# The six loads of batch 0's k move from SyncE's queue to ScalarE's

## The chip, the cores and the metric

The kernel runs on one core of a Trainium2 chip. The metric is the device time of one launch in microseconds, the median over runs. Six queues of work matter on the core: TensorE (PE, with its weight loads PEld), VectorE (DVE), ScalarE (ACT), GpSimd (POOL), SyncE (SP), which only issues DMAs, and the 16 DMA engines that all issued transfers share. ScalarE can issue DMAs too; an issue takes its place in ScalarE's own order of instructions.

## What is computed

Softcapped attention over 4 batches of 12 heads, 448 positions and 64 values per head, then a feed-forward block with a leaky activation on the 1792 tokens that come out:

```python
scores = scale * np.matmul(q, k.transpose(0, 1, 3, 2))
scores = cap * np.tanh(scores / cap)
scores = scores - np.max(scores, axis=-1, keepdims=True)
attn = np.exp(scores)
attn = attn / (np.sum(attn, axis=-1, keepdims=True) + 1e-09)
x = np.matmul(attn, v)            # heads side by side: 1792 x 768
h = x @ w_in                      # 768 x 2048
g = np.maximum(h, 0.0) + alpha * np.minimum(h, 0.0)
out = g @ w_out                   # 2048 x 768
```

q, k, v and cap are float32; w_in and w_out come in 8 bytes per value and are brought to float32 on the chip.

## The kernel before

Heads are worked on in pairs, six per batch. For batch 0 the q and k of each pair are loaded as 112 partitions of 2 x 256 values (`loads32`, line 467), 224 KB per load, into the tiles `wp4` to `wp7` (three pairs to a tile). TensorE turns them against the identity (line 543), ScalarE or VectorE copies the result out of PSUM (lines 425 and 427), and TensorE multiplies (scores, line 578). ScalarE then takes the tanh (line 615), VectorE the maximum of it (line 619), ScalarE the exponential (line 626), TensorE turns the result (line 730) and multiplies by v (line 793). Beside this, w_in comes in 16 chunks of 768 KB (issue at line 1048); VectorE brings each to float32 in three passes (lines 1060, 1064, 1070), it is scaled and split, and once all are there the first feed-forward product (line 959) can run, batch by batch, with the attention of the next batch between; the second product (line 1000) follows.

The order of all of this is made by a planner, `Plan`. Each step is handed to `op` with a priority, with its time on each engine that could do it, and with what it reads and writes. `order` (line 140) plays the program through with these times: each engine takes, of the steps that are ready, the one of lowest priority. Where TensorE has nothing ready it gets a small filler matmul on the identity (line 1235). `emit` (line 275) then calls the steps in this order, under a schedule in which every engine keeps the order it was given. So the order is fixed when the program is built, fillers included; at run time each instruction waits for what it needs.

A load is an `op` for SyncE alone, with an issue time, a delay and a transfer time of the planner's model (`load`, line 457). Its priority is a sum of a constant, of the pair, and of an entry of the list `OFF` (line 85) chosen by `plan.tag`: entries 155, 157, ... are those of k, and 156, 158, ... those of q, for pairs 0 to 5. This gives the order k of pair 1, k of pair 0, q of pairs 0, 1 and 3, then the first chunk of w_in, k of pairs 3 and 2, and then v, the rest of q and k, and further chunks of w_in mixed.

Before the planned part, ScalarE issues the load of `cap` into 128 partitions (line 1238, tile `small`), VectorE computes its reciprocal, and ScalarE loads two of the values into registers:

```python
nc.scalar.dma_start(out=capt, in_=cap.to_broadcast([P, 1]))
...
nc.scalar.load(capr, capt[:1].bitcast(I32))
nc.scalar.load(icapr, icap[:1].bitcast(I32))
all_ops()
with tc.manual_schedule():
    plan.emit()
```

Of the kernel before, what the change touches and what calls it, by code (L numbers as in the profile page):

```python
# [39 lines left out]
QK_P = -455.54  # L40
# [3 lines left out]
A_S = 17.19  # L44
# [43 lines left out]
class Handle:  # L88


    def __init__(self, kind):
        self.kind, self.ops, self.slot = kind, [], None


class Plan:
# [4 lines left out]

    def __init__(self):
        self.ops, self.acc, self.line = [], {}, []
        self.fill, self.fill_until = None, 0.0
        self.tag = -1

    def handle(self, kind):
# [5 lines left out]
    def op(self, prio, times, fn, r=(), w=(), rows=1.0, port=True, mode=0, first=0.0):  # L112
        o = lambda: None
        o.first = first
        o.prio, o.times, o.fn, o.rows, o.idx, o.port, o.mode = prio + OFF[self.tag], times, fn, rows, len(self.ops), port, mode
        o.handles, deps = [], set()
        for write, regions in ((False, r), (True, w)):
            for x in regions:
                if isinstance(x, Handle):
                    if x not in o.handles:  # L120
                        o.handles.append(x)
                        x.ops.append(o)
                    x = (x, 0, 1)
                space, lo, hi = x
                old = self.acc.setdefault(space, [])
                deps.update(e[2] for e in old if e[0] < hi and lo < e[1] and (write or e[3]))
                if write:
                    old[:] = [e for e in old if e[0] < lo or hi < e[1]]
        for write, regions in ((False, r), (True, w)):
            for x in regions:  # L130
                space, lo, hi = (x, 0, 1) if isinstance(x, Handle) else x
                self.acc[space].append((lo, hi, o.idx, write))
        o.deps = len(deps)
        o.next = []
        for d in deps:
            self.ops[d].next.append(o)
        self.ops.append(o)
        return o
# [134 lines left out]
        return started  # L273

    def emit(self):
        for _, fn, e in self.order():
            fn(e)

# [2 lines left out]
def kernel(  # L281
# [11 lines left out]
    nc = tc.nc  # L293
# [76 lines left out]
    plan = Plan()  # L370
    op = plan.op
# [82 lines left out]
    def heads(src, b, pair):  # L454
        return src[b, 2 * pair:2 * pair + 2].rearrange("h (p c) d -> p h (c d)", c=NCH)

    def load(prio, dst, src, b, pair, w):
        op(prio, {"sp": (600, 1400, 940)}, lambda e: nc.sync.dma_start(out=dst.rearrange("p (h c) -> p h c", h=2),
                                                          in_=heads(src, b, pair)), w=w)

    class Unit:
        pass
# [2 lines left out]
    raw32, qT, v0 = {}, {}, {}  # L465

    def loads32():
        for pair in range(NPAIR):
            n = 2 * NCH * D
            for i, src in ((4, k), (6, q)):  # L470
                o = pair % 3 * n
                t = wpair[i + pair // 3].rearrange("p a b -> p (a b)")[:CP, o:o + n]
                raw32[i, pair] = t, (("wp", i + pair // 3), o, o + n)
                qT[pair] = wpair[i + pair // 3].rearrange("p a b -> p (a b)")[:, o:o + S]
                plan.tag = 155 + 2 * pair + (i == 6)
                load(QK_P + A_S * pair, t, src, 0, pair, [raw32[i, pair][1]])
        vbatch(0)

    def vslot(b, pair):
# [24 lines left out]
    def vbatch(b):  # L504

        u = Unit()
        vb.append(u)
        t = vam[:, b % 2]
        u.vmx, u.inv, u.s = (t[:, NPAIR + i:NPAIR + i + 1] for i in range(3))
        u.osc, u.tok = small[:, 12 + b:13 + b], ("vam", b % 2)  # L510
        plan.tag = 142 + b
        prio = V_P if b == 0 else B1_P + (b - 1) * NPAIR * B_S - B_S
        op(prio, {"dve": 30}, lambda e: nc.vector.memset(t[:, :NPAIR], 0.0), w=[(u.tok, 0, 9)])
        tops = []
        for pair in range(NPAIR):
            rv, m = vslot(b, pair)
            v0[b, pair] = rv, m
            plan.tag = 167 + 6 * (b > 0) + pair if b < 2 else 142 + b
            load(prio + 0.4 * pair, rv, v, b, pair, [m])
            plan.tag = 142 + b  # L520
            if b < VM:
                tops.append((rv.bitcast(BF16).rearrange("p (c f t) -> p c f t", f=P, t=2), m))
                if len(tops) == (2 if b else NPAIR):
                    gram_v(prio + 0.4 * pair, t[:, pair:pair + 1], (u.tok, pair, pair + 1), tops)
                    tops = []
                continue
            op(prio + 0.4 * pair, {"dve": 680}, lambda e, pair=pair, rv=rv: absmax(t[:CP, pair:pair + 1], rv),
               r=[m], w=[(u.tok, pair, pair + 1)], port=False)
        prio += 3
        op(prio, {"dve": 80}, lambda e: nc.vector.tensor_reduce(out=u.vmx, in_=t[:, :NPAIR], axis=AX.X, op=ALU.max),  # L530
           r=[(u.tok, 0, 6)], w=[(u.tok, 6, 7)])
        first, *rest = pow2(u.inv, u.s, None)
        if b < VM:
            first, *rest = root(u.inv, lambda: nc.vector.reciprocal(out=u.s, in_=u.inv))
        allmax(prio, u.vmx, P, [(u.tok, 6, 7)], first, [(u.tok, 7, 9)])
        chain(prio, rest, w=[(u.tok, 7, 9)])
# [335 lines left out]
    def attention(b, pair, mate):  # L872
# [6 lines left out]
        for dst, src, w in ((rq, q, rqr), (rk, k, rkr)):  # L879
            if scores32:  # L880
                for h in range(2):
                    op(prio - 20, {"sp": LOAD_C}, lambda e, h=h, dst=dst, src=src: nc.sync.dma_start(
                        out=dst.rearrange("p (c h d) -> p h c d", h=2, d=D)[:, h],
                        in_=src[b, 2 * pair + h].rearrange("(p c) d -> p c d", c=NCH)), w=[(w[0], w[1] + h / 2, w[1] + (h + 1) / 2)])
            else:
                load(prio - 20, dst, src, b, pair, [w])
# [323 lines left out]
    def all_ops():  # L1210
        loads32()
        g_scales(2300)
        for part in range(2):
            attention_0(part)
        for j in range(0, NF, WG):
            w_in_chunks(j, WG)
        for part in range(2):
            mm1_batch(0, *PART[part], part)
        w_out_all()
        out_scale(0)  # L1220
        for b in range(1, B + 1):
            if b < B:
                vbatch(b)
                for pair in range(0, NPAIR, 2):
                    a = attention(b, pair, None)
                    units([a, attention(b, pair + 1, a)], S, ST1_P, finish)
                out_scale(b)
            mm2_batch(b - 1)
            if b < B:
                mm1_batch(b, 0, S, 0)  # L1230
# [52 lines left out]
```

## Time and profile before

| what | us |
|---|---|
| median of 3 runs | 666.45 (665.8 to 666.66) |
| the profiled execution's own time | 667.37 |
| its span, first to last instruction | 665.6 |

The profile is one execution recorded by the hardware profiler. A busy share of an engine is an average over the whole span, so the rows below are mostly of the first 60 us, where the loads in question are. A row of the timeline gives the start, the time taken (of the group, where like instructions were merged), and in brackets how long the engine was idle before it and what ended that. "SPq" and "ACTq" are issues of DMAs by those engines; the time of an issue is not the time of the transfer.

### The profile page before, as it was taken

Reading aid. Unit: us, or ns where it says so; the run is one execution under the profiler, and the core shown is the slowest. Engines: PE = TensorE matmul, PEld = TensorE weight load, DVE = VectorE, ACT = ScalarE, POOL = GpSimd, SP = SyncE. Lnnn points to the kernel's source line nnn. Section 1 sums busy time; section 2 is a strip of 40 time slices with the busy share of each in tenths; the row PEclk is TensorE's granted clock in tenths of the full one; section 3 lists DMA queues with packets and bytes.
Section 4 is the critical chain, followed back from the end, with each engine's and each line's share of the span. In section 5 each row is a group of like instructions: output and inputs, shape, how many; then the busy total and the mean of one; then the engine's idle time right before and its main releaser. Section 6 shows DMA issues by size and latency. Waiting matters only on the chain.

```text
span 665.6 us, 13056 instructions
## 1 busy us (share of the span) xinstructions
PE 642.9 (97%) x4934; PEld 406.2 (61%) x4934; DVE 469.8 (71%) x885; ACT 407.0 (61%) x839; POOL 245.8 (37%) x369
## 2 busy tenths in 40 slices
PE   9986999999999999999999999999999999999997
PEld 8864877888886655455455555544555555556664
DVE  3899999999999977989975877899994004440000
ACT  5876899988787877747853766778774113331000
POOL 1243457547764734635544321357451000000000
PEclk9997999999999999999999999999999999999999
DMA  9998863735753699948676899968667100000111
GB/s 221 286 274 231 258 188 103 225 107 151 148 89 63 156 164 197 169 99 157 116 156 155 162 175 178 185 120 165 113 116 131 33 19 24 1 1 1 37 35 25
DMA packets 190047, 87.05 MB, mean 131 GB/s; under 512 B 156256, under 2 KB 186272, under 8 KB 189984
## 3 DMA queue, kind: packets, MB, share of 16 engines
q1 hardware_dynamic: 189760, 86.12, 59.1%
q8 instruction: 39, 0.64, 0.4%
q14 instruction: 24, 0.20, 0.1%
q10 hardware_dynamic: 224, 0.10, 0.1%
HBM read 45.82 MB, written 5.51 MB: 77 GB/s over the span
## 4 chain that ended last, share of the span: by engine, by line
PE 55%; DMA 2%; DVE 2%; ACT 1%; issue 1%; SPq 0%; DVEq 0%; ACTq 0%
PE p L959 25%; PE p L1000 23%; PE p L776 4%; PE s L584 3%; DMA ptall<-pw 2%; DMA rqk<-in_k_dram 1%; DVE small L394 1%; DVE mxs L619 0%; DVE pw L441 0%; PE p L411 0%; ACT tall L626 0%; PE p L414 0%; DVE pw L435 0%; ACT tall L615 0%; DVE nat L438 0%
## 5 line engine op out<-in xcount | busy, mean ns | idle before, releaser
L959 PE MATMUL p<-xring,wi 128*128 128x448 f16 (+2 forms) x1440 | 224.3, 315 | 0.8 <-DVE iv_wi L388 0.8
L1000 PE MATMUL p<-wp,gall 128*128 128x384 f16 x1344 | 224.1, 326 | 0.1
L959 PEld LDWEIGHTS <-wi 128*128 128x128 f16 x1440 | 135.4, 98 | 83.7 <-issue 4.0
L1000 PEld LDWEIGHTS <-gall 128*128 128x128 f16 x1344 | 129.6, 98 | 89.9 <-issue 6.2
L626 ACT ACTIVATE tall<-tall,mxs 128x448 f32<-128x448 f32 x126 | 83.2, 666 | 18.9 <-POOL mxs L621 13.3
L969 DVE SCALAR_TENSOR_TENSOR gr<-p,ca_g,gr 128x448 f32<-128x448 f32 (+2 forms) x80 | 46.8, 585 | 52.5 <-ACT gr L431 51.7
L621 POOL TENSOR_SCALAR mxs<-mxs,small 128x2 f32<-128x2 f32 x70 | 43.6, 623 | 80.0 <-DVE mxs L619 66.8
L619 DVE TENSOR_REDUCE mxs<-tall 128x2 f32<-128x896 f32 x63 | 67.7, 1078 | 4.7 <-ACT tall L615 4.2
L441 DVE SCALAR_TENSOR_TENSOR pw<-tall,rr,pw 128x448 f16<-128x448 f32 x84 | 60.0, 725 | 8.6 <-ACT pw L431 7.9
L431 ACT ACTIVATE gr<-p,cs_g 128x448 f32<-128x448 f32 (+2 forms) x66 | 36.7, 557 | 37.1 <-PE p L959 36.0
L431 ACT ACTIVATE wp<-p,small 128x384 f32<-128x384 f32 x23 | 13.2, 576 | 62.2 <-PE p L1000 62.1
L615 ACT ACTIVATE tall<-s,ams 128x896 f32<-128x896 f32 x42 | 41.5, 999 | 12.3 <-PE s L584 5.7
L438 POOL TENSOR_TENSOR gall<-gr,gall 128x256 f16<-128x256 f32 (+4 forms) x50 | 37.2, 746 | 19.4 <-ACT gall L425 12.2
L645 POOL TENSOR_SCALAR rr<-sums 128x2 f32<-128x2 f32 (+2 forms) x70 | 23.1, 330 | 57.0 <-ACT tall L626 41.5
L425 ACT ACTIVATE gall<-gr 128x384 f16<-128x384 f32 (+4 forms) x58 | 26.6, 465 | 28.0 <-DVE gr L969 27.9
L435 DVE TENSOR_SCALAR wp<-p,joint 128x384 f32<-128x384 f32 (+1 forms) x2 | 1.0, 517 | 60.4 <-ACT wp L431 60.4
L431 ACT ACTIVATE pw<-tall,rr 128x448 f16<-128x448 f32 x46 | 30.3, 664 | 16.4 <-DMA ptall<-pw 9.9
L776 PE MATMUL p<-ptall,vs 112*64 112x448 f16 x384 | 39.4, 354 | 0.0
L438 DVE TENSOR_TENSOR gall<-gr,gall 128x384 f16<-128x384 f32 (+3 forms) x62 | 30.1, 486 | 4.7 <-ACT gall L425 1.8
L776 PEld LDWEIGHTS <-vs 112*64 112x64 f16 x384 | 21.2, 110 | 16.9 <-issue 5.1
L584 PE MATMUL s<-qkTs 64*128 64x448 f16 (+1 forms) x288 | 28.1, 352 | 0.6 <-ACT tall L615 0.6
L427 POOL CAST gall<-gr 128x192 f16<-128x192 f32 (+4 forms) x28 | 19.0, 681 | 24.4 <-DVE gr L969 22.5
(180 smaller groups left out, 943.3 us busy)
## 6 DMA issues: line engine op xcount, KB each, us to landing
wp<-in_moe_w_in_dram SPq DMA_DIRECT2D x16, 768.0 KB, 7.9
wp<-in_moe_w_out_dram SPq DMA_DIRECT2D x16, 768.0 KB, 4.9
rvs<-in_v_dram SPq DMA_DIRECT2D x38, 224.0 KB, 3.2
rqk<-in_k_dram SPq DMA_DIRECT2D x12, 224.0 KB, 3.2
rqk<-in_q_dram SPq DMA_DIRECT2D x12, 224.0 KB, 3.3
ptall<-pw SPq DMA_TRANSPOSE x128, 3.3
wp<-in_k_dram SPq DMA_DIRECT2D x6, 224.0 KB, 8.6
wp<-in_q_dram SPq DMA_DIRECT2D x6, 224.0 KB, 7.6
```

What stands on the lines that cost most here:

```text
L431: nc.scalar.activation(out=o, in_=i, func=AF.Copy, scale=s)
L438: (nc.gpsimd if e == "pool" else nc.vector).tensor_tensor(out=o, in0=a, in1=b, op=ALU.subtract)
L441: nc.vector.scalar_tensor_tensor(out=o, in0=i, scalar=s, in1=hi, op0=ALU.mult, op1=ALU.subtract)
L584: yield lambda z=z, w=w: nc.tensor.matmul(s[rows, x, :S], q[a, z * S + cols.start:z * S + cols.stop], q[a, w * S:(w + 1) * S], start=(z == ...
L615: op(pr, {"act": (152 if reg else 245) + 377 * 2}, lambda e: nc.scalar.activation(out=t, in_=s[:, :, :S].rearrange("p c (j k) -> p c j k", ...
L619: op(pr, {"dve": 136 + 469 * 2}, lambda e: nc.vector.tensor_reduce(out=mt, in_=t, axis=AX.XY, op=ALU.max), r=tr, w=[mr], port=False)
L621: op(pr, {"dve": 200, "pool": 265}, lambda e: (nc.gpsimd if e == "pool" else nc.vector).tensor_scalar(out=mt, in0=mt, scalar1=ncap, scalar ...
L626: nc.scalar.activation(out=t[:, x], in_=t[:, x], func=AF.Exp, scale=capr, bias=mt[:, x:x + 1], accum_out=sums[:, u.idx % 3, col + x:col + ...
L776: nc.tensor.matmul(pv[x * D:(x + 1) * D, :n], vs[:, z, c:c + D], u.pt[x][:CP, y * NCH + kc], start=(i == 0), stop=(i == len(prods) - 1))
L959: nc.tensor.matmul(ps_p[h.slot][:, :n], w[:, z, kk, :], x[:, d, o:o + n], start=(kk == 0 and z == d), stop=(kk == NPAIR - 1 and z == 1))
L969: op(pr, {"dve": 198 + 1.07 * n}, lambda e: nc.vector.scalar_tensor_tensor(out=t, in0=ps_p[h.slot][:, :n], scalar=ca_g[:, j:j + 1], in1=t, ...
L1000: nc.tensor.matmul(ps_p[h.slot][:, :NH], g[j][:, d, t * P:(t + 1) * P], w[:, z, hf * NH:(hf + 1) * NH], start=(j == 0 and z == d), stop=(j ...
```

## The change

The six `load` steps of k stay in the planner with the same priorities and times, but with no source, and such a step issues nothing. In their place a list `early` keeps six issues on ScalarE's queue, in the order of the pairs 0 to 5, and `emit` calls them ahead of all planned steps. On ScalarE they stand behind the load of `cap`, which is issued earlier.

```diff
-        self.fill, self.fill_until = None, 0.0
+        self.fill, self.fill_until, self.early = None, 0.0, []
...
     def emit(self):
+        for fn in self.early:
+            fn()
         for _, fn, e in self.order():
             fn(e)
...
     def load(prio, dst, src, b, pair, w):
-        op(prio, {"sp": (600, 1400, 940)}, lambda e: nc.sync.dma_start(out=dst.rearrange("p (h c) -> p h c", h=2),
-                                                          in_=heads(src, b, pair)), w=w)
+        op(prio, {"sp": (600, 1400, 940)}, lambda e: src is None or nc.sync.dma_start(
+            out=dst.rearrange("p (h c) -> p h c", h=2), in_=heads(src, b, pair)), w=w)
...
-                load(QK_P + A_S * pair, t, src, 0, pair, [raw32[i, pair][1]])
+                if i == 4:
+                    plan.early.append(lambda t=t, src=src, pair=pair: nc.scalar.dma_start(
+                        out=t.rearrange("p (h c) -> p h c", h=2), in_=heads(src, 0, pair)))
+                load(QK_P + A_S * pair, t, None if i == 4 else src, 0, pair, [raw32[i, pair][1]])
```

## Rows read from the trace of the kernel before

**Rows 1.** The page: busy time, share of the span and instructions of each engine.
```profile
PE 642.9 (97%) x4934; PEld 406.2 (61%) x4934; DVE 469.8 (71%) x885; ACT 407.0 (61%) x839; POOL 245.8 (37%) x369
```

**Rows 2.** TensorE by stretches: stretch, length, busy (instructions), granted clock, DMA share, GB/s.
```profile
5.00:10.00 5.00, 4.99 (x84) 1.00 1.12 282
...
62.00:160.00 98.00, 92.76 (x979) 1.00 0.55 166
160.00:260.00 100.00, 99.59 (x808) 1.00 0.72 135
```

**Rows 3.** Timeline of SyncE, the issues of the first 10 us.
```profile
0.72 0.91 SPq L458 DMA_DIRECT2D wp<-in_k_dram  x2
1.67 1.46 SPq L458 DMA_DIRECT2D wp<-in_q_dram  x3
3.17 0.46 SPq L1048 DMA_DIRECT2D wp<-in_moe_w_in_dram  x1
...
6.02 0.68 SPq L458 DMA_DIRECT2D wp<-in_q_dram  x1
...
8.85 2.88 SPq L1048 DMA_DIRECT2D wp<-in_moe_w_in_dram  x2
```

**Rows 4.** Single DMA issues, from issue to landing, in us: k1, cap, k0, q0, q3, w0.
```profile
wp<-in_k_dram SPq DMA_DIRECT2D x1, 224.0 KB, 2.9
small<-in_cap_dram ACTq DMA_DIRECT2D x1, 0.5 KB, 3.8
wp<-in_k_dram SPq DMA_DIRECT2D x1, 224.0 KB, 4.8
wp<-in_q_dram SPq DMA_DIRECT2D x1, 224.0 KB, 5.3
wp<-in_q_dram SPq DMA_DIRECT2D x1, 224.0 KB, 6.2
wp<-in_moe_w_in_dram SPq DMA_DIRECT2D x1, 768.0 KB, 8.1
```

**Rows 5.** Timeline of VectorE: the first chunk of w_in, the first maximum, the fifth chunk.
```profile
11.32 0.56 DVE L1060 TENSOR_SCALAR wi<-wp 128x768 int32<-128x768 int32 x1 [6.21 <-DMA wp<-in_moe_w_in_dram]
...
12.79 1.08 DVE L619 TENSOR_REDUCE mxs<-gall 128x2 f32<-128x896 f32 x1
...
33.04 0.56 DVE L1060 TENSOR_SCALAR wi<-wp 128x768 int32<-128x768 int32 x1 [0.44 <-DMA wp<-in_moe_w_in_dram]
```

**Rows 6.** Timeline of TensorE: five turns, the first scores, two later turns.
```profile
5.08 4.87 PE L543 MATMUL p<-ident,wp 112*64 112x112 f32 x80
9.88 1.78 PE L578 MATMUL s<-tall,wp 64*128 64x224 f32 x16
...
13.79 1.75 PE L543 MATMUL p<-ident,wp 112*64 112x112 f32 x32
```

**Rows 7.** Timeline of ScalarE up to its first tanh.
```profile
0.72 0.57 ACTq L1238 DMA_DIRECT2D small<-in_cap_dram  x1
1.32 1.28 ACT L425 ACT_TABLE_LOAD   x1 [1.32 <-PEq L1267]
6.40 0.54 ACT L425 ACTIVATE tall<-p 128x448 f32<-128x448 f32 x1 [3.79 <-PE p L543]
...
10.96 1.73 ACT L615 ACTIVATE gall<-s 128x896 f32<-128x896 f32 x2 [0.42 <-PE s L578]
```

**Rows 8.** As rows 2, one stretch of the head.
```profile
3.00:4.00 1.00, 1.00 (x13) 1.00 0.71 59
```

**Rows 9.** Waits of VectorE from 11 to 62 us: total us, times, longest.
```profile
DVE wi L1060 <- DMA wp<-in_moe_w_in_dram: 6.6, 2, 6.2
```

**Rows 10.** TensorE from 56 us: one stretch as in rows 2, eight transposes twice.
```profile
56.00:60.00 4.00, 3.88 (x19) 0.50 1.05 326
...
56.09 2.23 PE L730 MATMUL p<-ident,gall 128*112 128x128 f32 x8 [0.90 <-DVE xs L812]
...
61.24 1.08 PE L730 MATMUL p<-ident,gall 128*112 128x128 f32 x8
```

## The prediction, made before the change was run

> **What bounds the kernel now.** Read first the page's busy times: TensorE is busy for 97% of the span [rows 1]. By stage [rows 2], it is full from 5 to 10 us and again from 160 us on (99.59 of 100 us), and between 62 and 160 us it lacks only 5 us. So a delay at the head has little room to be swallowed later, and a gain at the head has to come out of a wait. Matmul time hides one thing: a busy TensorE in the first stretch is partly waiting on loads, because its ends are modelled. So read the loads next.
>
> SyncE issues, in the planner's order, k of pair 1, k of pair 0, q0, q1, q3, then the first chunk of w_in (call it w0), then the other k [rows 3]. The order follows from the priorities in the code (OFF from entry 155 on). Issue time plus time to landing [rows 4] gives: k1 at 0.72+2.9 = 3.6 us, k0 at 1.2+4.8 = 6.0, q0 at 1.67+5.3 = 7.0, q3 at 2.7+6.2 = 8.9, w0 at 3.17+8.1 = 11.3. From k0 to q3 three loads land in 2.9 us, so one load of 224 KB costs 0.95 us of the DMA engines, and w0 (768 KB) 2.4 us.
>
> Now who waits for those. TensorE's five first turns (80 matmuls, line 543) run from 5.08 us, and the first scores start at 9.88 [rows 6]. Two later turns, whose loads are there, take 1.75 us together, some 0.8 each (second start to first), or 4.1 us for five; here they take 4.8, spaced by the landings. VectorE's chain starts with w0: its first conversion stands idle for 6.21 us on that DMA and starts at 11.32, as w0 lands; its first reduction of scores stands behind it, at 12.79 [rows 5]. After that VectorE has hardly a gap up to 62 us, and the one that a DMA ends is 0.44 us at 33 us: the 6.6 us in the table of waits is 6.2 plus that [rows 5, 9]. So two landings set the head: the five q and k loads for TensorE and w0 for VectorE; and the DMA engines are the resource behind both, moving 282 GB/s at a share above 1 from 5 to 10 us [rows 2].
>
> **The change part by part.** The planner still sees all loads with their old times (the call on SyncE merely does nothing), so the order on TensorE, VectorE and GpSimd and the filler matmuls stay. What moves is six issues, and with them the order in which 1.3 MB come in.
>
> *Issuing.* SyncE spends about 0.46 us per issue (0.91 for two, 1.46 for three [rows 3]); it loses six. This gains nothing: from its eighth DMA on, SyncE is not short of time but waits for a landing eight DMAs back. The issue at 6.02 starts as k0 lands (6.0), and the one at 8.85 follows q3 (8.9) likewise; six in a row do so, from 6.02 to 12.20 [rows 3, 4]. ScalarE gains six issues: 6 x 0.46 = 2.8 us behind its load of cap, which ends at 1.29. Behind them stand its table load (1.28 us) and then the first copy of a turn, at 6.40 [rows 7]. Without waits it is ready at 1.29+2.8+1.28 = 5.4 us, under the cover of that idle time. If the loads of the two queues take turns in the count of eight, the last k load waits for a landing near 8 us and ScalarE is ready near 9.8; the first turn will by then end near 9 (next step), so this costs 0 to 0.8 us on ScalarE, which catches up over five copies of 0.54 us against turns of 0.8. I take 0. If the six k loads come first in the count, q1 waits for cap's landing (0.72+3.8 = 4.5) and q3 for one near 6; the bytes ahead of w0 are then the same.
>
> *The five loads of the first turns.* ScalarE's queue brings pair 0 before pair 1, both behind cap. Up to 4.1 us little arrives: from 3 to 4 us the rate is 59 GB/s, while cap is in flight and lands at 4.5 [rows 4, 8]. Then k0 and k1 share the engines with the rest of q1 and with q3: four loads at 0.95 = 3.8 us, so k1 lands near 7.9. Bounds: 6.0 if ScalarE's queue goes first (two loads), 9 if SyncE's does. The first turn moves from 5.08 to 8.0, five turns at 0.8 follow without a wait, and the scores start near 12.1 instead of 9.88: +2.2 us (bounds +0.3 and +3.2).
>
> *w0.* It was sixth; now, while it comes in, the other queue delivers k2 to k5. With equal shares about three of the four pass before w0 is complete: 11.3 + 3 x 0.95 = 14.2 us, +2.9. Bounds: all four, 15.1; or none and, with k1 and k0 also behind it, 9.4. I take 14.2, as nothing in the rows favours a queue. [...]
>
> *What it does to the end.* The first reduction needs the tanh of the scores and stands behind two conversions of w0. Through TensorE: 12.1 + 2.0 (before: scores 9.88, tanh from 10.96 to some 11.9) = 14.1 [rows 6, 7]. Through VectorE: 14.2 + 1.5 (12.79 less 11.32) = 15.7. VectorE decides: +2.9. Given back later: waits whose end does not move. At 33.04 VectorE waits 0.44 us for a chunk of w_in; by then all twelve k and q loads are in as before, so it lands as before and the wait is gone [rows 5]. The other gaps end on TensorE or GpSimd, which are late themselves. So +2.9 - 0.4 = +2.5 us at 62 us, and TensorE has nothing after it that would swallow it [rows 2].
>
> **The rivals.**
> (a) *The delay is swallowed, or w0 is hardly late.* If SyncE's queue gets most of the engines until w0 is in, w0 keeps to about 11.3; then TensorE alone is late, by 2 to 3 us at the scores, and VectorE by 14.1 - 12.79 = 1.3 less the 0.44. Or part goes into TensorE's 5 us of waits between 62 and 160. Against it: those waits are on VectorE and ScalarE, which come late too. Time: +0 to +1, about 667.0.
> (b) *Faster.* Place: the poor stretch from 3 to 4 us. If one queue alone leaves the engines idle there, a second fills it: 1 us is about one load of 0.95, so k1 still lands by 5.1, and with SyncE's q0, q1, q3 two places earlier the scores start near 9.3. If w0 also keeps its two places (9.4), the tanh decides: 11.3 instead of 12.79, -1.5 us, 664.9. It decides from the point where k1 lands before 5.1 and w0 before 9.8. Against it: cap's packets stand on that very queue ahead of k, and the engines are full from 5 us on.
> (c) *Dearer.* TensorE now stands idle from about 5.1 to 8 us behind its fillers. After the idle stretch before 56 us the granted clock was 0.50 from 56 to 60, the lower level, and eight transposes took 2.23 instead of 1.08 us [rows 10]. If it falls so at the head, turns and scores take about twice as long for some 4 us: +2 on TensorE's path, 14.1 to 16.1, which is 0.4 over VectorE's 15.7; and the scores' own copies and tanh on ScalarE, which then has its table load late as well, may add the two turns of 0.8 that it is behind. Time: 666.45 + 2.5 + 0.4 + 1.6 = 671.0.
> (d) *It does not do what it says.* The k loads may be held on ScalarE behind the register loads of cap (which need VectorE's work at 5 us). Then k1 lands near 8 all the same and w0 near 12 to 14: +2 to +3, inside the forecast's range.
>
> **How the numbers follow.** The profiled execution took 667.37 us, 0.92 above the median of 666.45; the forecast adds 2.5 us to either: 669.9 for its like, 669.0 for the median. About 0.2% (1.3 us) can be told from no change, so faster means under 665.1 and slower over 667.8. Forecast, (d) included: 0.54, between 667.4 and 670.4, of which 0.05 under 667.8. (a) 0.21, nearly all within 0.2%. (b) 0.10. (c) 0.15. So slower 0.49 + 0.15 = 0.64, and 0.01 from (a) = 0.65; same 0.05 + 0.20 = 0.25; faster 0.10. The range takes in the forecast, (a) and most of (c): 665.8 to 671.4.
>
> **What would show it.** Right: k1 lands near 8 us and the first turn of line 543 starts then; w0 lands near 14 and line 1060 on VectorE starts with it; the wait at 33 us is gone; the scores of all later stages stand 2 to 3 us later. Wrong: line 1060 still starts near 11.3 (the shares are not equal), the first turn starts before 6 (cap does not hold the queue), or the delay is there at 40 us and gone at 160 (TensorE had room after all).

## The result, and the profile after

The changed kernel took 670.92 us (median of 7 runs, 669.96 to 675.03) beside 665.8 us (664.32 to 667.2, 7 runs) for the kernel before: a ratio of 1.0089 with a 95% interval of 1.0069 to 1.0108, that is 4.6 to 7.2 us, and 5.1 by the medians. The profiled execution took 670.85 us, its span is 668.9. Slower, then, and by about twice the 2.5 us of the forecast. (Lines of kernel.py behind the last edit stand 5 lower: the turns are line 548, the scores 583, the tanh 620, the first conversion of w_in 1065, the maximum 624, the fillers 1240. Between the first edit and the last they stand 2 lower: ScalarE's copies are line 427. The k issues of ScalarE are line 479.)

Start with single DMA issues, as in [rows 4]: from issue to landing, in us, for cap, k0, k1 and w0.

```profile
small<-in_cap_dram ACTq DMA_DIRECT2D x1, 0.5 KB, 4.2
...
wp<-in_k_dram ACTq DMA_DIRECT2D x1, 224.0 KB, 6.3
...
wp<-in_k_dram ACTq DMA_DIRECT2D x1, 224.0 KB, 7.4
...
wp<-in_moe_w_in_dram SPq DMA_DIRECT2D x1, 768.0 KB, 11.3
```

cap lands at 4.94, k0 (issued at 1.35) at 7.67, k1 (1.99) at 9.35, w0 (2.17) at 13.44. In between SyncE's queue brings q1 at 6.33 and q3 at 8.22. k1, which TensorE needs first, was there at 3.6 us before and is now the last of the five.

ScalarE, as in [rows 7]: its six issues take 5.35 us, because the last three wait in the count of eight that both queues share, for the landings of cap, q0 and q1. q0 was in at 3.48; the other two cost time (the fourth issue starts at 4.96, as cap lands, the sixth at 6.36, as q1 does). The table load follows and is done at 8.0, before the first turn has begun.

```profile
0.73 0.58 ACTq L1243 DMA_DIRECT2D small<-in_cap_dram  x1
1.34 5.35 ACTq L479 DMA_DIRECT2D wp<-in_k_dram  x6
6.73 1.28 ACT L427 ACT_TABLE_LOAD   x1 [6.73 <-DMA wp<-in_q_dram]
11.20 0.54 ACT L427 ACTIVATE tall<-p 128x448 f32<-128x448 f32 x1 [3.19 <-PE p L548]
12.70 0.54 ACT L427 ACTIVATE tall<-p 128x448 f32<-128x448 f32 x1 [0.95 <-PE p L548]
```

TensorE, as in [rows 6]: the first turn stands at 9.39 instead of 5.08, after 4.24 us without work, and the scores at 16.30 instead of 9.88.

```profile
1.45 3.70 PE L1240 MATMUL p<-ident 128*128 128x128 f16 x33 [1.45 <-POOL ident masks.py:199]
9.39 6.97 PE L548 MATMUL p<-ident,wp 112*64 112x112 f32 x80 [4.24 <-DMA wp<-in_k_dram]
16.30 1.78 PE L583 MATMUL s<-tall,wp 64*128 64x224 f32 x16
18.01 1.35 PE L1240 MATMUL p<-ident 128*128 128x128 f16 x21
```

The 80 matmuls take 6.97 us although all five loads are there by 9.35. The stretches of TensorE, with the columns of [rows 2], say why: from 10 to 15 us the granted clock is 0.50. (The first fillers of the program run at half pace too: 33 in 3.70 us, while 21 of the same form take 1.35 us at 18.01. The trace's first clock record stands at 5.19, in the profile before at 5.69, and the clock column shows 1.00 ahead of it, so that 1.00 is not a measurement.)

```profile
5.00:10.00 5.00, 0.76 (x8) 0.86 1.11 279
10.00:15.00 5.00, 5.00 (x58) 0.50 1.12 291
15.00:20.00 5.00, 5.00 (x77) 0.96 1.10 313
62.00:160.00 98.00, 92.99 (x947) 0.98 0.60 181
370.00:410.00 40.00, 39.96 (x289) 1.00 0.96 180
```

VectorE, as in [rows 5]: w0 is converted at 13.47, 2.15 us later than before. Yet the first maximum, at 18.32, is 5.53 later, and what it waits for 3.30 us is the tanh on ScalarE, so in the end TensorE. The wait at 33 us is gone.

```profile
13.47 0.56 DVE L1065 TENSOR_SCALAR wi<-wp 128x768 int32<-128x768 int32 x1 [7.90 <-DMA wp<-in_moe_w_in_dram]
14.06 0.96 DVE L1069 SCALAR_TENSOR_TENSOR wi<-wp,wi 128x768 int32<-128x768 int32 x1
18.32 1.09 DVE L624 TENSOR_REDUCE mxs<-gall 128x2 f32<-128x896 f32 x1 [3.30 <-ACT gall L620]
```

Since TensorE runs the same 4934 matmuls in the same order in both kernels, the two traces can be laid side by side, instruction by instruction. I call *offset* the start of an instruction of TensorE less that of the same instruction in the profile before. It is +6.41 at the scores, +6.32 at 33 us, +5.86 at 39 (0.46 given back where VectorE waited before), +5.87 at 63, +5.84 at 240 and +5.96 at 365. Then it falls to +3.33 at 405, and stays so to the end. That is the one place where a delay is swallowed in this profile. Before, TensorE has waits there, on VectorE and ScalarE:

```profile
370.00:410.00 40.00, 37.74 (x255) 1.00 1.03 193
...
376.63 0.26 PE L411 MATMUL p<-ident,small 112*2 112x112 f32 x1 [0.96 <-DVE small L394]
391.42 0.26 PE L411 MATMUL p<-ident,small 112*2 112x112 f32 x1 [0.73 <-DVE small L394]
403.56 0.76 PE L584 MATMUL s<-qkTs 64*64 64x448 f16 x12 [0.57 <-ACT tall L615]
```

These three are 2.26 us; after, TensorE is busy for 39.96 of the 40 us.

### The profile page after: what moved, and what is told of

Read it like the earlier page. It is cut to its first block, busy times and chain, and to the rows that moved or that the text cites. A ratio compares the mean times of both kernels' runs of the same rounds, so it can differ in the third digit from the quotient of the medians.

```text
span 668.9 us, 13054 instructions
## 1 busy us (share of the span) xinstructions
PE 644.9 (96%) x4934; PEld 408.8 (61%) x4934; DVE 467.3 (70%) x885; ACT 406.9 (61%) x839; POOL 246.8 (37%) x369
## 4 chain that ended last, share of the span: by engine, by line
PE 58%; DVE 1%; issue 0%; ACT 0%; ACTq 0%
PE p L1005 26%; PE p L964 25%; PE p L781 4%; PE s L589 3%; DVE mxs L624 0%; PE p L413 0%; PE p L416 0%; DVE small L396 0%; DVE xring L443 0%; DVE pw L443 0%; DVE vam L396 0%; DVE xring L437 0%; DVE pw L437 0%; ACT wp L433 0%; DVE wp L437 0%
```

## The experiments

The theory after the result had three parts: (1) k1 lands late because it stands behind cap and k0 on one queue; (2) the granted clock of 0.50 that followed the idle stretch of 4.24 us makes the turns long; (3) w0, though displaced, is covered. The rivals were the ones of the prediction: w0 on VectorE decides, or the other k loads take its bandwidth. A table of all kernels stands at the end of this section.

### TensorE kept busy through the idle stretch

```diff
     def emit(self):
         for fn in self.early:
             fn()
+        for _ in range(72):
+            self.fill(3)
```

> The changed kernel with 72 more filler matmuls ahead of the first turn, so that TensorE stays busy until pair 1's k lands at 9.35 us. Theory (the dear part is the clock that fell in TensorE's idle stretch): the first turn still starts near 9.4, the five turns take 4.1 instead of 6.9 us, the scores start near 13.5 instead of 16.3, and all later matmuls stand 2.3 to 2.8 us behind the kernel before instead of 5.9. Rival (the late loads alone cost all of it, the clock nothing): still 5.9 behind.

671.12 us beside 666.19 of before, which the next three experiments share (ratio 1.0073, 1.0044 to 1.0101). The loads land as in the changed kernel, the first turn starts at 9.62, and the turns take 4.05 us:

```profile
9.62 4.05 PE L550 MATMUL p<-ident,wp 112*64 112x112 f32 x80
...
10.00:15.00 5.00, 5.00 (x92) 1.00 1.12 286
```

So the fallen clock costs 6.97 - 4.05 = 2.9 us at the head, and the offset at 63 us is 3.17 instead of 5.87. The time, however, hardly moved. I come back to this with the two last runs.

### The needed load first among the six

```diff
-        for fn in self.early:
-            fn()
+        for i in (1, 0, 2, 3, 4, 5):
+            self.early[i]()
```

> The changed kernel with pair 1's k issued ahead of pair 0's on ScalarE's queue, as SyncE had them. Theory: k of pair 1 lands near 7.7 us, the first turn starts there, 2.5 us after the fillers end instead of 4.2. If the clock still falls, the scores start near 14.6 and the later matmuls are 4.3 us behind the kernel before; if 2.5 us of idling leave it up, the scores start near 12.6, the first chunk of w_in decides, and they are 1.7 us behind. Rival (the order of the two does not matter, only the last of the five loads): 5.9 behind as in the changed kernel.

671.52 us (1.0095, 1.0061 to 1.0128). k1 lands at 7.97, the first turn follows, the clock falls nonetheless, and the offset at 63 us is 4.64:

```profile
8.02 7.12 PE L548 MATMUL p<-ident,wp 112*64 112x112 f32 x80 [3.29 <-DMA wp<-in_k_dram]
...
10.00:15.00 5.00, 5.00 (x62) 0.56 1.13 272
```

The order among the six is worth 1.2 us at the head against this profile of the changed kernel, and 0.4 against its second one further down (5.07), which is less than can be told. With either order k1 stands behind cap, and an idle stretch of 3.29 us was followed by the lower clock.

### Only the four later k on ScalarE

```diff
-                if i == 4:
+                if i == 4 and pair > 1:
```

(and the same condition where `load` is given no source)

> Only k of pairs 2 to 5 goes to ScalarE's queue; k of pairs 0 and 1 stays on SyncE's, in its old places. Theory (bytes that overtake cost what they displace): the first turn starts at 5.1 as before, the turns are spaced by landings, the last of the five lands near 11.8 and the scores start near 12.7; the first chunk of w_in lands near 15 and the later matmuls are 3.4 us behind the kernel before. Rival (all comes from the two loads that TensorE waits for first): 0 to 0.5 us behind.

672.83 us (1.0081, 1.0046 to 1.0117). The first turn starts at 5.08 as before, but now the turns are spaced by the landings, and each keeps the pace of a single turn at 21.02 us in the kernel before, 0.99 us:

```profile
5.08 0.99 PE L548 MATMUL p<-ident,wp 112*64 112x112 f32 x16
6.93 0.99 PE L548 MATMUL p<-ident,wp 112*64 112x112 f32 x16 [0.86 <-DMA wp<-in_k_dram]
9.10 0.99 PE L548 MATMUL p<-ident,wp 112*64 112x112 f32 x16 [1.18 <-DMA wp<-in_q_dram]
10.54 0.99 PE L548 MATMUL p<-ident,wp 112*64 112x112 f32 x16 [0.46 <-DMA wp<-in_q_dram]
13.38 0.99 PE L548 MATMUL p<-ident,wp 112*64 112x112 f32 x16 [1.85 <-DMA wp<-in_q_dram]
```

The scores start at 14.30, and w0, which lands at 15.63, is as late as they are. This is a second mechanism that the change contains: k loads that nobody needs yet take a share of the engines, and places in the count of eight, from q loads that are needed. The issue of q3 waited until 5.54 for cap's landing, eight DMAs back, and landed at 13.25.

### Only the two first k on ScalarE

```diff
-                if i == 4:
+                if i == 4 and pair < 2:
```

(and the same condition where `load` is given no source)

> Only k of pairs 0 and 1 goes to ScalarE's queue; the other four stay on SyncE's, in their old places. Theory (TensorE's start decides: pair 1's k behind cap and pair 0's k): the first turn starts near 9 us with the clock down, the first chunk of w_in lands near 11.3 as before, and the later matmuls are still 5 to 5.9 us behind the kernel before. Rival (the displaced first chunk of w_in decides, as forecast): 0 to 1 us behind.

671.35 us (1.0079, 1.0051 to 1.0107). This is nearly the whole change at the head: k1 behind cap and k0, an idle stretch, the lower clock, offset 5.21 at 63 us.

```profile
9.15 6.55 PE L548 MATMUL p<-ident,wp 112*64 112x112 f32 x80 [4.44 <-DMA wp<-in_k_dram]
...
10.00:15.00 5.00, 5.00 (x64) 0.57 1.13 258
```

w0 is converted at 11.64, only 0.32 us later than before. Had VectorE decided, this kernel would have lost almost nothing. So the rival that puts the loss on w0 falls.

### cap taken out of the way, before and after

Both leave out the load of cap and use the constant 30.0 in its place.

```diff
-    nc.scalar.dma_start(out=capt, in_=cap.to_broadcast([P, 1]))
+    nc.vector.memset(capt, 30.0)
```

> The kernel before with the load of cap left out: its tile is filled with the constant 30.0 instead (the value that the input has). Theory (cap's 128 rows of 4 bytes slow everything from 3 to 4 us): the rate in that stretch is over 200 GB/s instead of 59, pair 0's k lands near 4.6 us instead of 6.0, the first chunk of w_in near 9.9 instead of 11.3, and the later matmuls stand 1.0 to 1.4 us ahead of the kernel before. Rival (the poor stretch belongs to the start of a queue's transfers, cap or not): within 0.3 us of the kernel before.

> The changed kernel with the load of cap left out: its tile is filled with the constant 30.0 instead. Theory (cap stands ahead of k on ScalarE's queue and holds it): pair 1's k lands near 7.3 us instead of 9.35, TensorE idles some 2 us instead of 4.2, and the later matmuls are 1.5 us behind the kernel before if the clock stays up, 3.5 to 4 if it falls. Rival (cap does not matter, k is late because the two queues share the engines): 5.5 to 5.9 behind as in the changed kernel.

In the kernel before, 666.56 us (1.0006, 0.9979 to 1.0032). The poor stretch from 3 to 4 us of [rows 8] is filled, so it was cap's: 265 GB/s in place of 59.

```profile
3.00:4.00 1.00, 1.00 (x13) 1.00 0.89 265
```

k0 lands at 4.15 instead of 6.0, and the scores start 1.11 us earlier, but w0 landed at 12.63 in this execution, and the first maximum, which comes right behind w0's conversions, is 1.34 us later than before:

```profile
14.13 1.08 DVE L619 TENSOR_REDUCE mxs<-gall 128x2 f32<-128x896 f32 x1
```

The offset is +0.61 at 33 us, +0.15 at 39 and +1.58 at 63; the last step arises near 48 us, and the run with two k loads ahead of cap, below, shows where it comes from. The gain at the head was not kept, and the run says nothing on what it would be worth.

In the changed kernel, 668.47 us (1.0037, 1.0014 to 1.0061), 2.6 us above the 665.83 of before. k1 lands at 6.71, TensorE idles for 1.59 us, its clock stays at 1.00:

```profile
6.75 4.05 PE L548 MATMUL p<-ident,wp 112*64 112x112 f32 x80 [1.59 <-DMA wp<-in_k_dram]
...
10.00:15.00 5.00, 5.00 (x79) 1.00 1.13 274
```

The scores start only 0.85 us late, the offset is 0.44 at 63 us. cap ahead of k on the same queue, and what followed from it, was 5.87 - 0.44 = 5.4 us of the head (4.6 by the second profile of the changed kernel). The time is still 2.6 us above that of before, by an interval of 0.9 to 4.1. In this profile another 1.2 us were lost between 365 and 405 us, where TensorE waits for ScalarE, VectorE and a DMA; why it waits longer there was not taken apart.

Here too the maximum comes right behind the conversions of w0 (landed at 12.91), 1.61 us later than before:

```profile
14.40 1.08 DVE L624 TENSOR_REDUCE mxs<-gall 128x2 f32<-128x896 f32 x1
```

The offset at 33 us is 0.89. So in the two kernels without cap, where w0 does set the maximum, 0.7 us of its delay does not reach TensorE (1.34 and 0.61, 1.61 and 0.89).

### The kernel before once more

No edit.

> The kernel before, once more, for a second profile. The profile at hand has TensorE lose 2.3 us between 370 and 410 us, where the changed kernel's has none of it. If that loss differs from one execution to the next, it is smaller or gone here and all stages up to 365 us agree within 0.1 us; if it belongs to the kernel before, it is there again.

666.19 us. The head repeats to 0.2 us at the scores, but w0 landed at 10.18 instead of 11.30; at 63 us the offset is -0.57 and after 405 us -1.20. The first profile is thus that of an execution 1.2 us longer than this one, and the offsets at the end of all other kernels are 1.2 us larger when they are counted from this one. The expected agreement was too narrow: a single profile carries about 1 us of chance, most of it from 370 to 410 us, where this execution lost 1.5 us of TensorE and the first one 2.3. Offsets below 1 us are not read as effects here.

### All six k on ScalarE, but two of them ahead of cap

```diff
-        for fn in self.early:
+        for fn in self.early[2:]:
             fn()
...
+    all_ops()
+    plan.early[1]()
+    plan.early[0]()
     nc.scalar.dma_start(out=capt, in_=cap.to_broadcast([P, 1]))
...
-    all_ops()
```

> All six k loads on ScalarE's queue as in the changed kernel, but pair 1's k first, then pair 0's, then cap, then the other four: TensorE's first loads are no longer behind cap. This leaves the forecast's own term alone, the first chunk of w_in displaced by k of pairs 2 to 5. Theory: pair 1's k lands near 5 us, TensorE does not idle enough for the clock to fall, the scores start near 10.4 (0.5 late), the first chunk of w_in lands near 13.5 to 14 instead of 11.3, VectorE's first reduction is 2 to 2.7 us late, and the later matmuls stand 1.5 to 2.3 us behind the kernel before. Rival (the displaced chunk is swallowed, all of the loss was TensorE's start): 0 to 0.5 behind.

666.93 us beside 666.35 (1.0007, 0.999 to 1.0025): the loss is gone. k1 lands at 4.66, q1 and k0 at 6.12 and 6.36, cap at 7.63, and w0 at 11.53 in spite of k2 to k5 on the other queue.

```profile
5.08 0.99 PE L548 MATMUL p<-ident,wp 112*64 112x112 f32 x16
6.41 3.29 PE L548 MATMUL p<-ident,wp 112*64 112x112 f32 x64 [0.33 <-DMA wp<-in_k_dram]
9.62 1.78 PE L583 MATMUL s<-tall,wp 64*128 64x224 f32 x16
...
11.55 0.56 DVE L1065 TENSOR_SCALAR wi<-wp 128x768 int32<-128x768 int32 x1 [3.30 <-DMA wp<-in_moe_w_in_dram]
```

The theory that went into this run wanted w0 at 13.5 to 14, and that falls: with cap in the middle of the queue, only k2 (10.58) landed between cap and w0, not three k. As w0 was not displaced, the run does not say what a displaced w0 costs. The same six loads on the same second queue cost 5.1 us by the medians (4.5 in the second series below), or nothing that can be told, by what stands in front of k1.

### Only those two on ScalarE, ahead of cap

The edit above, with `pair < 2` as in the fourth experiment.

> Only k of pairs 1 and 0 on ScalarE's queue, in this order and ahead of cap; the other four stay on SyncE's in their old places. Theory: nothing that was needed later overtakes anything, and nothing stands behind cap, so the five loads and the first chunk of w_in land as before within 0.5 us and the later matmuls stand within 0.6 us of the kernel before. Rival (a second busy queue costs by itself): 1.5 us or more behind.

667.46 us (1.0011, 0.9992 to 1.003). w0 is converted at 10.66, the scores start at 10.15, the offset is -0.28 at 40 us and +1.11 at 63. That second number arises near 48 us, far from what was changed, as in two other executions (the kernel before without cap, and only the four later k). In these three the granted clock falls once more than in the kernel before, at 44.6, 45.4 and 49.5 us; over the whole span it is 0.991 in this profile and 0.992 in the two others, beside 0.994. From 44 to 48 us, this run and then the kernel before:

```profile
44.00:48.00 4.00, 3.49 (x28) 0.57 1.15 297
...
44.00:48.00 4.00, 3.49 (x54) 1.00 1.13 327
```

The offset steps up by 1.6 us in each of the three, where that stretch lies; whether their edits bring it about is not shown. No loss and no gain that can be told.

### Needed loads first on both queues

ScalarE issues k1, q0 and cap, in this order; SyncE issues k0, q1, q3, w0 and all others.

```diff
-                if i == 4:
+                if (i, pair) in ((4, 1), (6, 0)):
...
+    all_ops()
+    plan.early[1]()
+    plan.early[0]()
     nc.scalar.dma_start(out=capt, in_=cap.to_broadcast([P, 1]))
```

(and the calls in `emit` left out)

> A version that might beat the kernel before: the five loads that TensorE needs first are dealt out to the two queues in the order of need. ScalarE's queue takes k of pair 1, q of pair 0, then cap; SyncE's takes k of pair 0, q of pairs 1 and 3, the first chunk of w_in and the rest in their old order. Theory: the first two k land near 4.5 us, all five by 7.7, the turns run without a wait and the scores start near 9.3 instead of 9.9; the first chunk of w_in lands near 10.7 instead of 11.3; the later matmuls stand 0.3 to 0.6 us ahead of the kernel before, a gain of under 0.1%. Rival (the head's gain is lost in VectorE's and the transfers' later waits, as in the other runs with two queues): between 0.3 ahead and 1.2 behind.

664.9 us beside 665.87 (0.9994, 0.9972 to 1.0016). The five turns run without a gap, and both the scores and w0 are 0.9 us earlier than in the first profile of before (0.7 us earlier and 0.2 us later than in the second):

```profile
4.88 4.15 PE L546 MATMUL p<-ident,wp 112*64 112x112 f32 x80
8.96 1.78 PE L581 MATMUL s<-tall,wp 64*128 64x224 f32 x16
...
10.44 0.56 DVE L1063 TENSOR_SCALAR wi<-wp 128x768 int32<-128x768 int32 x1 [1.95 <-DMA wp<-in_moe_w_in_dram]
```

The profile's offset is -1.36 at 63 us and -1.87 at the end, 0.8 and 0.7 us ahead of the second profile of before. The interval of the runs does not confirm that as a gain.

### The changed kernel again, and again with the fillers

No new edit; both on one chip, to settle what the clock costs at the end.

> The changed kernel unaltered, a second profile and more times on the same chip as the next run. If its head is a property of the kernel, the first turn starts at 9.4 +- 0.3 us, the granted clock from 10 to 15 us is near 0.50, and TensorE's matmuls at 60 us stand 5.9 +- 0.5 us later than before; time 1.0089 +- 0.002 of before. If the fallen clock was an accident of one execution, the clock is 1.00 and the offset near 3.2.

> The changed kernel with 72 further filler matmuls at the start, a second time, beside the unaltered changed kernel. Theory A, the fallen clock costs 2.7 us that last to the end: the time is 2 to 3.4 us below that of the run beside it, and the profile's offset at 60 us is near 3.2 and stays. Theory B, most of it is given back later in any case (the earlier profile showed the offset grow from 3.2 to 4.2 us by 210 us): the time is 0.5 to 1.7 us below. Theory C, it costs nothing at the end: within 0.5 us.

Beside 666.2 of before: 670.74 us (1.0073, 1.0046 to 1.01) without the fillers, 671.09 (1.0075, 1.005 to 1.0101) with them. The turns without:

```profile
9.12 6.44 PE L548 MATMUL p<-ident,wp 112*64 112x112 f32 x80 [3.97 <-DMA wp<-in_k_dram]
...
10.00:15.00 5.00, 5.00 (x66) 1.00 1.13 278
...
10.93 0.54 ACT L427 ACTIVATE tall<-p 128x448 f32<-128x448 f32 x1 [2.69 <-PE p L548]
12.43 0.54 ACT L427 ACTIVATE tall<-p 128x448 f32<-128x448 f32 x1 [0.95 <-PE p L548]
```

and with:

```profile
10.26 4.05 PE L550 MATMUL p<-ident,wp 112*64 112x112 f32 x80
...
11.29 0.54 ACT L429 ACTIVATE tall<-p 128x448 f32<-128x448 f32 x1 [3.61 <-PE p L550]
12.06 0.54 ACT L429 ACTIVATE tall<-p 128x448 f32<-128x448 f32 x1 [0.22 <-PE p L550]
```

Without fillers a turn is copied every 1.50 us, with them every 0.77: the slow turns repeat, though in this execution the clock column shows 1.00. Its trace holds no clock record before 14.06 us, where one of 1.00 begins, so the column says nothing of the turns; the last 11 fillers ahead of the wait, from 3.77 us, take 1.38 us, still the slow pace of the first ones. The offset at 63 us, 5.07, is outside the 5.9 +- 0.5 that was expected; the first turn and the time are inside theirs. With the fillers k1 is in at 9.18, but the fillers themselves last until the first turn at 10.26, so they give 1.1 us of what they save back at once (0.3 us in the first run with them).

At 63 us the filled kernel is 5.07 - 3.71 = 1.4 us ahead. At 365 us it is 1.1 ahead (6.35 and 5.23), at 405 it is 1.1 behind (4.34 and 5.43), and the times agree within 0.4 us. The first pair did the same: 2.7 ahead at 63 us, 1.8 at 365, 0.9 behind after 405, times 0.2 apart. So theory A, the full price at the end, falls. Theory C, nothing at the end, fits best, but with 6 runs each that spread over 3 us the lower part of B is not excluded. Where it goes is seen: most of it from 365 to 405 us, where the changed kernel gives back 2.0 and 2.6 us and the filled one nothing. Why it does so is not: the waits of TensorE there end on VectorE (0.96 and 0.73 us in the first profile before) and ScalarE (0.57; 1.4 and 1.2 in the filled ones), and no run here takes that stage apart.

### All kernels

Offsets of TensorE in us, of one profile each against the first profile before (the 72 extra fillers left out of the count), and the ratio of the times.

| kernel | first turn | scores | offset at scores | at 63 us | at 365 us | at the end | ratio |
|---|---|---|---|---|---|---|---|
| needed first on both queues | 4.88 | 8.96 | -0.92 | -1.36 | -1.52 | -1.87 | 0.9994 |
| before, again | 5.08 | 9.69 | -0.19 | -0.57 | -0.44 | -1.20 | - |
| all six, two ahead of cap | 5.08 | 9.62 | -0.26 | -0.51 | -0.29 | -0.76 | 1.0007 |
| changed, without cap | 6.75 | 10.74 | +0.85 | +0.44 | +0.46 | +1.61 | 1.0037 |
| two only, ahead of cap | 5.08 | 10.15 | +0.27 | +1.11 | +1.50 | +1.67 | 1.0011 |
| before, without cap | 4.79 | 8.77 | -1.11 | +1.58 | +2.26 | +0.37 | 1.0006 |
| changed, fillers | 9.62 | 13.60 | +3.72 | +3.17 | +4.14 | +4.23 | 1.0073 |
| changed, fillers, again | 10.26 | 14.24 | +4.36 | +3.71 | +5.23 | +5.43 | 1.0075 |
| changed, k1 first of the six | 8.02 | 15.07 | +5.18 | +4.64 | +4.84 | +5.10 | 1.0095 |
| changed, again | 9.12 | 15.49 | +5.61 | +5.07 | +6.35 | +4.34 | 1.0073 |
| only the four later k | 5.08 | 14.30 | +4.42 | +5.17 | +5.46 | +5.14 | 1.0081 |
| only the two first k | 9.15 | 15.63 | +5.75 | +5.21 | +5.43 | +5.11 | 1.0079 |
| changed | 9.39 | 16.30 | +6.41 | +5.87 | +5.96 | +3.33 | 1.0089 |

The table falls into two groups. Scores less than 1 us late, and the ratio stays under 1.004; of these only the changed kernel without cap has an interval that leaves out 1. Scores 3.7 us late or more, and it lies between 1.0073 and 1.0095, with intervals that overlap. A late start of the scores goes with the loss in all seven, whatever made it late. How late does not show: 3.7 and 6.4 us give the same time, and why is open.

## Why the prediction was right or wrong

*Direction and range.* Slower was right. The forecast of +2.5 us was half of the 5.1 that came; 670.9 lies within the range only because the range took in most of rival (c). The step that failed is "VectorE decides: +2.9": w0 was covered, and TensorE's path, put at +2.2 at the scores, was +6.41. Two of its terms were too small, the landing of k1 and the five turns. The landing is the one that the times bear out: with the clock kept up by fillers the scores are still 3.7 us late, and the time is 4.9 us longer all the same. The slow turns make the rest of the delay at the scores, and no run shows them in the time.

*Issuing: right.* The loads of the two queues take turns in the count of eight, ScalarE is ready at 8.0 (9.8 in the prediction) under the cover of a first turn that starts at 9.39, and the cost is 0. SyncE had no use for the issue time saved: its issue behind w0's starts at 7.68, as k0 lands (7.67). Nor did the second queue bring a higher rate: from 5 to 10 us 279 GB/s after, 282 before [rows 2].

*The five loads of the first turns: mechanism right, size off.* cap does hold the queue, k1 does come fourth behind it. But k1 landed at 9.35 (9.08 the second time), not 7.9, just beyond the upper bound of 9. From cap's landing on, q1, k0, q3 and k1 took 9.35 - 4.94 = 4.4 us, not the 3.4 of the sum (7.9 less cap's 4.5). The sum let these four have the engines to themselves; yet by 9.35 us SyncE's queue had moved 1017 KB, 345 more than q0, q1 and q3 together, and ScalarE's 115 KB more than k0 and k1. So w0 and k2 took 460 KB of the engines' work ahead of k1, where the sum had nothing. (The sum also starts at 4.1 us, ahead of cap's landing, and no row gives that start.) The step failed there, and with cap 0.4 later the first turn came 1.4 later than forecast.

*Five turns at 0.8: wrong.* They took 6.97 us, at the lower clock. This is rival (c), with a chance of 0.15. The prediction had the row that shows it [rows 10] and the idle stretch, "from about 5.1 to 8 us", and still took the clock to stay up; no reason excluded the fall, so it should have been the main case. Its price on TensorE was put at 2 us, and 2.4 to 2.9 were measured (6.44 and 6.97 less 4.05). The two terms together explain the scores: 12.1 + 1.4 + 2.9 = 16.4, measured 16.30. That the 671.0 of (c) meets the measured 670.92 is luck: it stands on w0's 2.5 us, adds 0.4 for TensorE and 1.6 for ScalarE's copies, and w0 was covered, ScalarE was ready in time, and the turns' price does not show at the end.

*w0, and "VectorE decides": wrong.* w0 landed at 13.44, near the forecast of 14.2 (of k2 to k5 two landed ahead of it, not three), and it was covered: the maximum waited 3.30 us for the tanh. It would have been covered with the clock up as well: with the fillers the maximum, at 15.62, still waited 0.78 us for the tanh. A second run shows the loss without a late w0: with k0 and k1 alone on ScalarE, w0 was nearly on time and the loss was the same. And where w0 did set the maximum, without cap, 0.7 us of its delay did not reach TensorE, a slack that the prediction, which passed on all but 0.4, did not have. No run here has w0 late by 2 us or more with the scores on time. With cap left out, the landings of the two queues alternate: q0 4.64, k0 4.94, q1 5.96, k1 6.71, q3 8.00, k2 8.46.

*Given back at 33 us: right.* 0.44 was forecast, 0.46 measured.

*Nothing after 62 us that would swallow it: right to 365 us, wrong after.* The offset lies between 5.83 and 6.09 us from 39 to 365 us. But the stretches that were read ended at 260 us, and the waits of 2.3 us from 370 to 410 were not seen; there 2.6 and 2.0 us were given back in the two profiles of the changed kernel, and nothing in those of the filled one.

*The rivals.* (a) and (b) did not come, for the reasons stated against them. (b) has its point all the same: k1 by 5.1 and w0 before 9.8 was its condition, and the kernel with the needed loads first on both queues reaches 4.84 and 10.42 and shows the most negative offset at 63 us, -1.36 beside the -0.57 of the kernel before run again, a difference below what is read as an effect here. (d) is excluded: ScalarE's first k issue starts at 1.34.

*What stays open.* Why, in the filled kernels, the 1.4 to 2.7 us won at the head are lost again; why the changed kernel without cap is still 2.6 us slower; why the loss of TensorE from 370 to 410 us differs from execution to execution (2.3 and 1.5 us in the same kernel); and whether the last reordering is a gain.

## What to carry to other kernels

The second issuing queue brought no bandwidth here (279 GB/s beside 282); it changed the order of arrival. Ask first what stands ahead of the load that is needed first on its new queue, and which unneeded loads now share the engines with the needed ones. A tiny load was the thing in the way here: cap's 0.5 KB ahead of k1, and what followed from it, were 4.6 to 5.4 us of the head. And where an engine that will be waiting is TensorE, look in the profiles at its pace after waits as long: here five turns took 6.44 to 7.12 us after 3.29 to 4.44 us of idling, and 4.05 after 1.59. Look too whether that price lasts: here it was 2.4 to 2.9 us at the head and did not show in the time.

## What the runs showed of the hardware

- While the load of cap, 0.5 KB into 128 partitions, comes first on its queue, little else arrives: 59 GB/s from 3 to 4 us with it [rows 8], 265 without. Issued third, behind two loads of 224 KB, it is felt less: in the three kernels that do so the lowest rate after 3 us is 164 to 202 GB/s, from 6 to 7 us. A load of 224 KB that stands behind it on its queue landed 2.7 us after it (k0), one ahead of it on the same queue at 4.66 us.
- After TensorE had idled for 3.29, 4.24 and 4.44 us at the head, the granted clock from 10 to 15 us was 0.56, 0.50 and 0.57, and the five turns took 7.12, 6.97 and 6.55 us. After 1.59 us it was 1.00, and they took 4.05; with four idle pieces of at most 1.85 us between them each turn took 0.99. After 3.97 us of idling the five took 6.44 us, but that execution has no clock record before 14.06 us.
- The program's 33 first fillers, from 1.45 us, follow each other every 107 ns, and 21 later ones of the same form (from 11.60 us in the kernel before, 18.01 in the changed one) every 56.
- In one execution the turns ran at half pace (1.50 us a turn instead of 0.77) while the clock column showed 1.00, which it also does where the trace has no record. The pace of like instructions is the safer reading of the two.
- In three profiles the clock fell once more than in the kernel before, at 44.6, 45.4 and 49.5 us (from 44 to 48 us 0.57 beside 1.00 with the two first k alone ahead of cap), and the offset steps up by 1.6 us there.
- The same kernel twice gives offsets of up to 1.2 us at the end, and the second profile of the changed kernel lost 1.3 us between 240 and 270 us that the first did not lose. One profile does not settle an effect of 1 us at the end of this kernel, though TensorE's first 20 us repeat to 0.3 us in the kernel before and to 0.8 in the changed one. The landing of w0 repeats to 1.1 us in the kernel before (11.30 and 10.18).
